# Loads of the first pairs of heads, batch 0: six transfers issued by ScalarE instead of SyncE

## The chip, the cores and the metric

The kernel runs on one core of a Trainium2 chip. The metric is the device time of one execution in microseconds. Before the change the median is 187.37 us over 14 runs (185.96 to 188.53).

The engines are named as in the profile: PE is TensorE (matmuls), DVE is VectorE, ACT is ScalarE, POOL is GpSimd, SP is SyncE. SP computes nothing: it issues transfers. ACT both computes and can issue transfers. Each engine works through its own list of instructions in order; engines wait for each other, and for transfers, on semaphores.

## The reference

Four batches of eight heads of attention, sequence 768, head dimension 64, are followed by a dense block. Some heads ("retrieval") use the full causal mask, the others see only the first 4 keys and a window of 64.

```python
scores = scale * np.matmul(q, k.transpose(0, 1, 3, 2))
stream_keep = causal & (is_sink | in_win)
mask = np.where(retr[0, :, 0, 0, None, None], full_mask, stream_mask)
scores = np.where(mask[None, :, :, :], scores, -1000000000.0)
a = np.exp(scores - max);  a = a / (sum(a) + 1e-09)
attn_out = np.matmul(a, v)
x = attn_out.transpose(0, 2, 1, 3).reshape(B * S, H * D)     # 3072 x 512
h1 = x @ w1;  h2 = x @ w2;  g = np.maximum(h1, h2)           # 512 -> 1024
out = g @ w_out                                              # 1024 -> 512
```

(The lines are shortened; what is computed is unchanged.) The maximum of h1 and h2 is computed in the kernel as h2 + relu(h1 - h2). The part h2 @ w_out is x @ (w2 @ w_out), with the product of the two weights formed once, in the first 40 us or so.

## The kernel before

Heads are first sorted so that the retrieval heads come first; the permutation is computed from `is_retrieval` on DVE and loaded into registers of SP, POOL and ACT, so that a transfer can address "the head in slot s". Heads are then worked on in pairs: four pairs for each of four batches, sixteen rounds in all, numbered r.

For each pair, `pair(b, p)` (from line 658) issues six transfers into three float buffers: q, k and v, each with one transfer for each head. In batch 0 only half of each V is loaded there, because the other half of all heads is fetched at the very start by three transfers from ACT into `v_half` (line 321). A q or k transfer moves 192 KB, a half V transfer 96 KB, and a quarter of a weight 512 KB. After the loads, q and k are cast to bf16 (`qb`, line 301), transposed by PE through PSUM (`mm`, line 695) and copied into `qk` (again line 301). In batch 0 each transposed tile is copied in two halves, one by ACT and one by DVE. V is cast into `vb`. `attend` then makes score tiles on PE (line 578; in batch 0 PE also adds the masks, line 586), exponentials on ACT (line 599), and the product with V on PE (line 623), which DVE normalises. The dense block of a batch (`x_turn`, `dense`) follows its four pairs, interleaved with the next batch's attention.

Weights are loaded by `load_weight` (line 303). `EARLY` names one quarter of w_out that ACT issues at the start (line 324); the other three quarters of w_out and all of w1 and w2 are issued by SP (line 426).

The order of everything is made by a planner in Python, `Plan.schedule`. Each operation has a cost for each engine that may do it, a priority and dependencies; the planner gives every operation an engine and a start time, sorts by start time, and emits each engine's list in that order. The six loads of a pair are operations for the engine "SP" at 0.55 us each. The list of an engine is therefore fixed when the program is built.

Transfers issued by SP and ACT signal their landing on semaphores that are given out in turn from a set of eight. An issue that takes a semaphore over waits on its own engine until the transfer that had it before has landed.

Of the kernel before, what the change touches and what calls it, by code (L numbers as in the profile page):

```python
# [188 lines left out]
def kernel(  # L189
# [19 lines left out]
    nc = tc.nc  # L209
# [87 lines left out]
    def copy(e, o, i):  # L297
        if e == "ACT":
            nc.scalar.copy(out=o, in_=i)  # L299
        else:  # L300
            issued[e].append((V if e == "DVE" else nc.gpsimd).tensor_copy(out=o, in_=i).ins)  # L301
# [75 lines left out]
    def run(full, head, col, exact):  # L377
        P = Plan(*((SHIFT, HOLD) if exact else ({}, {})))
# [276 lines left out]
        def tok(t):  # L655
            return t.rearrange("c (p n) -> c p n", n=NB)

        def pair(b, p):
            r = b * HP + p
            s0 = 2 * p  # L660
            if p == 0:
                xs[b], xt[b], xt_ops[b], norms[b] = Buf(xs_p), Buf(xt_p), [], ([], [])
            raws, loads = [], []
            for i, src in enumerate((q, k, v)):
                t = Buf(ld)
                raws.append(t)
                order, rate = ("(p n)", WIDE) if wide[r] and src is not v else ("(n p)", NARROW)
                two = []
                n0 = NB // 2 if b == 0 and src is v else 0
                for h in range(2):  # L670
                    two.append(P.op(lambda e, t=t, src=src, h=h, order=order, n0=n0: nc.sync.dma_start(
                        out=t.t[:, h, n0:], in_=src[b, bass.ds(head(s0 + h), 1), 128 * n0:].rearrange(
                            f"o {order} d -> p (o n) d", p=128)),
                        {"SP": 0.55}, (), [t], prio=r + 0.01 * i, size=0.0983 if n0 else 0.197, rate=rate))
                loads.append(two)
            qk, vb = Buf(qk_p), Buf(vb_p)
            tk, cast = [], []
            qb = Buf(qb_p)
            for i in range(2):
                one_ = []  # L680
                for hs in ((0,), (1,)) if b == 0 else ((0, 1),):
                    def f(e, i=i, hs=hs):
                        for h in hs:
                            copy(e, qb.t[:, i, :, h, :], raws[i].t[:, h])
                    one_.append(P.op(f, {"POOL": 0.48, "DVE": 0.38} if b == 0 else {"POOL": 0.95},
                                     [loads[i][h] for h in hs], [raws[i], qb], prio=r + 0.01 * i, shared=True))
                cast += one_
                if not wide[r]:
                    continue
                bk = Buf(mm_p)  # L690

                def tr(e, i=i, bk=bk):
                    psb = bk.t[:, 0].bitcast(BF16)
                    for n in range(NB):
                        nc.tensor.transpose(psb[:, n * 128:(n + 1) * 128],  # L695
                                            qb.t[:, i, n].rearrange("p h d -> p (h d)"), ident)
                o = P.op(tr, {"PE": 0.34}, one_, [qb, bk, qk], prio=90 + 2 * r)
                for p0, p1 in ((0, 64), (64, 128)) if b == 0 else ((0, 128),):
                    w = (p1 - p0) / 128
                    tk.append(P.op(lambda e, bk=bk, i=i, p0=p0, p1=p1: copy(  # L700
                        e, tok(qk.t[:, i])[:, p0:p1],
                        bk.t[:, 0].bitcast(BF16)[:, 0:S].rearrange("c (n p) -> c p n", p=128)[:, p0:p1]),
                                   {"DVE": 0.1 + 0.8 * w, "ACT": 0.1 + 0.65 * w}, [o], [bk, qk], prio=r))
            if not wide[r]:
                tk.append(P.op(lambda e: nc.sync.dma_start_transpose(
                    out=qk.t.rearrange("c i (n p) -> c (i n) p", p=128),
                    in_=qb.t.rearrange("p i n h d -> p (i n h d)")),
                    {"SP": XBAR}, cast, [qb, qk], prio=r - 0.5, size=0.393, rate=0.2))
            n0 = NB // 2 if b == 0 else 0
            ov = []  # L710
            if b == 0:
                def fh(e):
                    for h in range(2):
                        copy(e, vb.t[:, h, 0:n0, 0:D], v_half[:, bass.ds(head(s0 + h), 1)].rearrange(
                            "p o (n d) -> p (o n) d", d=D))
                ov.append(P.op(fh, {"POOL": 0.6, "ACT": 0.6}, bufs=[v_held, vb], prio=r + 0.04, ready=DMA_FIRST + 5.2))

            def fv(e):
                for h in range(2):
                    copy(e, vb.t[:, h, n0:, 0:D], raws[2].t[:, h, n0:])  # L720
            ov.append(P.op(fv, {"POOL": 0.58, "DVE": 0.48} if b == 0 else {"POOL": 0.95}, loads[2],
                           [raws[2], vb], prio=r + 0.05, shared=True))

            last[0] = attend(b, p, qk, vb, tk, ov, r)
# [80 lines left out]
        for b in range(B):  # L805
            for p in range(HP):
                pair(b, p)
            x_turn(b)
            dense(b)
# [8 lines left out]
        order = P.schedule()  # L818
# [66 lines left out]
```

The softmax here doesn't subtract the row's maximum and nothing guards it: scores larger than these inputs give would overflow.

## Time and profile before

| | |
|---|---|
| median of 14 runs | 187.37 us |
| profiled execution | 187.53 us |
| its span, first to last instruction | 185.7 us |
| mean granted TensorE clock | 0.970 |
| busy PE / ACT / DVE / POOL | 171.8 / 115.9 / 86.9 / 50.4 us |
| SP: first q load issued, last half V of pair 0 issued | 4.86 us, 8.22 us (end) |
| ACT: three V transfers and one w_out quarter issued | 0.76 to 3.56 us |

Times in the timeline are microseconds from the first instruction of the span: the start, then how long it took, then engine, line and operation, output and input tile, and in brackets the idle time of the engine before it and what ended that. An engine named with a q (SPq, ACTq) is its queue issuing a transfer: the time shown is the issuing, not the transfer. When an operation's bracket names a DMA, its start tells when that transfer had landed. In the table of stages, the clock of PE is a share of its full speed, and the DMA share is how much of the time the core's 16 DMA engines were moving packets.

### The profile page before, as it was taken

The page shows a single profiled execution, that of the slowest core. Times are in us where ns is not written, and L with a number is a line of the kernel's source. Part 1 is how long each engine was busy: PE and PEld are TensorE (multiplying, and loading weights), DVE is VectorE, ACT ScalarE, POOL GpSimd, SP SyncE. Part 2 cuts the span into 40 slices and gives each one's busy share as a digit, 9 for nine tenths or more (in the row PEclk, how much of TensorE's full clock was granted, in tenths as well). Part 3 has the DMA queues.
Part 4 walks back from the last instruction along what each step waited for, and adds up shares of the span by engine and source line. Part 5 has one row for each costly group of instructions (what it writes and reads, how often), then busy time and mean ns, then how long its engine had stood idle before and what let it go on. Part 6 is the DMA issues. An engine that isn't in the chain of part 4 may idle for free.

```text
span 185.7 us, 4614 instructions
## 1 busy us (share of the span) xinstructions
PE 171.8 (93%) x1663; PEld 100.7 (54%) x1663; DVE 86.9 (47%) x250; ACT 115.9 (62%) x195; POOL 50.4 (27%) x108
## 2 busy tenths in 40 slices
PE   0769988899999999999999999999999999999990
PEld 0735754756665655664565456446555545545460
DVE  5647676868678586534378165354743000000000
ACT  2537898978888678817894386368844624426330
POOL 2201151375985764623025234100000000000000
PEclk9965799999999999999999999999999999999999
DMA  6999999999999999999999999982016612022032
GB/s 149 303 278 357 268 308 350 290 311 324 297 291 249 214 236 217 219 238 189 263 247 174 271 219 219 285 223 92 4 58 190 94 60 113 0 79 91 4 113 71
DMA packets 79553, 36.96 MB, mean 199 GB/s; under 512 B 68642, under 2 KB 73506, under 8 KB 79522
## 3 DMA queue, kind: packets, MB, share of 16 engines
q1 hardware_dynamic: 76130, 35.27, 77.3%
q10 hardware_dynamic: 3392, 1.31, 2.6%
q8 instruction: 15, 0.25, 0.6%
q14 instruction: 16, 0.13, 0.2%
HBM read 25.17 MB, written 6.29 MB: 169 GB/s over the span
## 4 chain that ended last, share of the span: by engine, by line
PE 84%; DMA 3%; ACT 3%; DVE 2%; SPq 1%; issue 1%; POOL 0%
PE mm L786 13%; PE mm L762 12%; PE sc L578 9%; PE po L623 9%; PE po L762 8%; PE mm L793 6%; PE po L786 6%; PE sc L786 4%; DMA ld<-in_q_dram 3%; PE mm L463 3%; PE po L793 3%; PE sc L762 2%; PE sc L793 2%; PE mm L695 2%; ACT at_all L599 2%; PE sc L586 2%
## 5 line engine op out<-in xcount | busy, mean ns | idle before, releaser
L599 ACT ACTIVATE at_all<-sc 128x1024 bf16<-128x1024 f32 (+2 forms) x72 | 59.8, 869 | 7.6 <-PE sc L578 3.5
L301 POOL CAST qb<-ld 128x384 bf16<-128x384 f32 x51 | 24.4, 510 | 24.0 <-DVE at_all L610 18.4
L762 PEld LDWEIGHTS <-wd_bf 128*128 128x128 bf16 x256 | 23.2, 98 | 13.8
L623 PE MATMUL po<-vb,at_all 128*128 128x65 bf16 x472 | 26.8, 198 | 0.1
L623 PEld LDWEIGHTS <-at_all 128*128 128x128 bf16 x472 | 22.0, 100 | 9.0 <-issue 1.2
L762 PE MATMUL mm<-xt,wd_bf 128*128 128x384 bf16 x136 | 26.8, 326 | 0.0
L578 PE MATMUL sc<-qk 64*128 64x128 bf16 (+2 forms) x364 | 23.5, 243 | 2.0 <-POOL qk L301 0.8
L642 DVE TENSOR_TENSOR xs<-po,rz 128x192 f32 x64 | 22.9, 357 | 2.9 <-DVE rz L639 0.6
L786 PEld LDWEIGHTS <-raw 128*128 128x128 bf16 x152 | 14.2, 98 | 13.8
L578 PEld LDWEIGHTS <-qk 64*128 64x128 bf16 x364 | 12.7, 95 | 14.9 <-issue 10.2
L301 POOL CAST vb<-ld 128x384 bf16<-128x384 f32 (+1 forms) x30 | 13.5, 479 | 23.3 <-DMA ld<-in_v_dram 9.8
L786 PE MATMUL mm<-wo_bf,raw 128*128 128x512 bf16 (+1 forms) x80 | 19.4, 368 | 0.0
L639 DVE RECIPROCAL rz<-po 128x6 f32<-128x6 f32 x32 | 6.2, 193 | 27.3 <-PE po L623 27.2
L762 PE MATMUL po<-xt,wd_bf 128*128 128x384 bf16 x92 | 18.1, 326 | 0.0
L299 ACT COPY ot<-mm 128x512 f32<-128x512 f32 (+1 forms) x12 | 6.8, 569 | 13.2 <-PE mm L793 11.6
L610 DVE TENSOR_TENSOR at_all<-at_all,smk 128x1024 bf16<-128x1024 bf16 (+3 forms) x27 | 15.0, 574 | 0.0
L793 PEld LDWEIGHTS <-xt 128*128 128x128 bf16 x100 | 9.3, 98 | 9.3
L793 PE MATMUL mm<-wm_bf,xt 128*128 128x512 bf16 (+1 forms) x56 | 13.9, 371 | 0.0
L610 DVE TENSOR_TENSOR at_all<-at_all,tri 128x256 bf16<-128x256 bf16 (+1 forms) x36 | 8.8, 278 | 6.7 <-ACT at_all L599 6.6
L695 PEld LDWEIGHTS <-qb 128*128 128x128 bf16 x108 | 7.5, 105 | 5.3 <-DVE qb L301 3.0
L299 ACT COPY vb<-vb 4x256 bf16<-4x256 bf16 (+1 forms) x16 | 6.1, 380 | 6.2 <-PE po L623 6.1
L770 ACT ACTIVATE raw<-mm 128x384 bf16<-128x384 f32 x17 | 8.4, 491 | 2.5 <-PE mm L762 2.2
(91 smaller groups left out, 190.6 us busy)
## 6 DMA issues: line engine op xcount, KB each, us to landing
ld<-in_q_dram SPq DMA_DIRECT2D x32, 192.0 KB, 4.6
ld<-in_k_dram SPq DMA_DIRECT2D x32, 192.0 KB, 4.7
out_dram<-ot SPq DMA_DIRECT2D x23, 256.0 KB, 2.3
ld<-in_v_dram SPq DMA_DIRECT2D x24, 192.0 KB, 4.5
raw<-in_moe_w_dram SPq DMA_DIRECT2D x8, 512.0 KB, 6.8
raw<-in_moe_w_out_dram SPq DMA_DIRECT2D x3, 512.0 KB, 6.0
xt<-in_v_dram ACTq DMA_DIRECT2D x3, 256.0 KB, 3.3
ld<-in_v_dram SPq DMA_DIRECT2D x8, 96.0 KB, 4.4
```

The lines of the kernel that those rows point to most:

```text
L299: nc.scalar.copy(out=o, in_=i)
L301: issued[e].append((V if e == "DVE" else nc.gpsimd).tensor_copy(out=o, in_=i).ins)
L578: nc.tensor.matmul(sc.t[:, k, off:off + w], lhsT=qk.t[64 * h:64 * h + 64, 1, j * 128:(j + 1) * 128], rhs=qk.t[64 * h:64 * h + 64, 0, q0:q0 ...
L599: nc.scalar.activation(out=a.t[:, k:k + m, 0:n], in_=sc.t[:, k:k + m, 0:n], func=ACT.Exp, scale=scale, bias=0.0 if bias is None else bias[ ...
L610: issued["DVE"].append(V.tensor_mul(out=y, in0=y, in1=z).ins)
L623: nc.tensor.matmul(po[u].t[:, 0, o:o + D + 1], lhsT=a.t[:, k, off + t * 128:off + (t + 1) * 128], rhs=vb.t[:, h, j, :], **fresh(u))
L642: V.tensor_tensor(out=xs[b].t[:, n0:n0 + nn, bass.ds(col(s0 + h), D)], in0=p4[:, i, :, 0:D], in1=rz_[:, i].unsqueeze(2).to_broadcast([128, ...
L695: nc.tensor.transpose(psb[:, n * 128:(n + 1) * 128], qb.t[:, i, n].rearrange("p h d -> p (h d)"), ident)
L762: nc.tensor.matmul(bk.t[:, 0, 0:GT], lhsT=wd_bf[:, c, f * 128:(f + 1) * 128], rhs=xt[b].t[:, g * NB // NG:(g + 1) * NB // NG, c, :], start ...
L770: nc.scalar.activation(out=gt.t[:, f, :], in_=bk.t[:, 0, 0:GT], func=ACT.Relu)
L786: nc.tensor.matmul(bk.t[:, 0, 0:m1 - m0], lhsT=gt.t[:, f, t * 128:(t + 1) * 128], rhs=wo_bf[:, f, m0:m1], start=(f == 0), stop=False)
L793: nc.tensor.matmul(bk.t[:, 0, 0:m1 - m0], lhsT=xt[b].t[:, c0 // 128, c, :], rhs=wm_bf[:, c, m0:m1], start=False, stop=(c == KC - 1))
```

## The change

In batch 0, the two k transfers of pair 0 and the two V transfers each of pairs 0 and 1 are issued by ACT; all other loads of pairs stay with SP. The planner still counts all of them as SP work at 0.55 us, so its plan is the same, and each issue is put into ACT's list where the plan's start time places it. The lines below the edit move by one.

```diff
                 n0 = NB // 2 if b == 0 and src is v else 0
+                queue = nc.scalar if b == 0 and (src is v and p < 2 or src is k and p == 0) else nc.sync
                 for h in range(2):
-                    two.append(P.op(lambda e, t=t, src=src, h=h, order=order, n0=n0: nc.sync.dma_start(
+                    two.append(P.op(lambda e, t=t, src=src, h=h, order=order, n0=n0, queue=queue: queue.dma_start(
                         out=t.t[:, h, n0:], in_=src[b, bass.ds(head(s0 + h), 1), 128 * n0:].rearrange(
                             f"o {order} d -> p (o n) d", p=128)),
                         {"SP": 0.55}, (), [t], prio=r + 0.01 * i, size=0.0983 if n0 else 0.197, rate=rate))
```

The words of the change also name w_out as issued by SyncE. The diff has no line for this: three quarters of w_out were issued by SP before, and the quarter in `EARLY` is issued by ACT before and after.

In ACT's list of the changed program the six issues stand as follows: the two k transfers and the first V transfer of pair 0 come ahead of the conversions of `v_half`; the second V transfer of pair 0 between the conversions for pair 0 and those for another pair, ahead of the conversion of the early w_out quarter; the two V transfers of pair 1 between ACT's copy of its half of the transposed q of pair 0 and its copy of its half of the transposed k of pair 0. The second V transfer of pair 0 takes over the semaphore of the first k transfer; the first V transfer of pair 1 that of the first V transfer of pair 0; the second V transfer of pair 1 that of the w_out quarter which SP issues behind pair 0's q.

## The prediction

> **What bounds the kernel now.** I read the slices of the page first, then busy time by stage, then the timeline of the first 21 us engine by engine, then the waits of the DMA queue and the chain.
>
> ```profile
> PE   0769988899999999999999999999999999999990
> PEclk9965799999999999999999999999999999999999
> DMA  6999999999999999999999999982016612022032
> ```
>
> ```profile
> 5.00:10.00 5.00, 3.71 (x43) 3.36 (x40) 2.90 (x12) 2.49 (x7) 1.08 (x2) 1.00 0.96 292
> 10.00:15.00 5.00, 3.71 (x30) 1.97 (x30) 2.76 (x7) 2.44 (x4) 0.00 (x0) 0.58 0.97 300
> 15.00:20.00 5.00, 4.58 (x50) 3.24 (x48) 3.34 (x9) 3.29 (x4) 1.16 (x3) 0.50 1.08 340
> 20.00:25.00 5.00, 5.00 (x73) 3.53 (x72) 3.74 (x12) 4.64 (x9) 1.74 (x6) 0.90 0.87 236
> 25.00:30.00 5.00, 3.58 (x51) 2.19 (x51) 3.60 (x9) 4.60 (x10) 1.64 (x4) 1.00 1.00 350
> 60.00:100.00 40.00, 40.00 (x431) 22.84 (x430) 23.72 (x66) 28.35 (x49) 16.97 (x37) 1.00 1.13 226
> ```
>
> The columns are PE, PEld, DVE, ACT, POOL busy, then granted clock, DMA share and GB/s. From about 31 us to the end PE never pauses and its order is fixed, so whatever the start loses or gains up to there is paid one for one at the end; nothing behind can absorb it. Between 20 and 30 us ACT is full (9.24 of 10 us). Between 12 and 20 us PE is full at half clock: a mean of 0.58, 0.50 and 0.90 means half clock from 10.8 to 21.0 us. DMA is full from 5 us on.
>
> ```profile
> 2.69 0.87 ACTq L310 DMA_DIRECT2D raw<-in_moe_w_out_dram  x1
> 5.88 1.11 ACT L299 CAST vb<-xt 128x192 bf16 x4 [0.80 <-DMA xt<-in_v_dram]
> 7.73 1.04 ACT L299 CAST wo_bf<-raw 128x1024 bf16<-128x1024 f32 x1 [0.74 <-DMA raw<-in_moe_w_out_dram]
> 9.75 0.48 ACT L299 COPY qk<-mm 128x384 bf16<-128x384 bf16 x1 [0.97 <-PE mm L695]
> 11.49 0.48 ACT L299 COPY qk<-mm 128x384 bf16<-128x384 bf16 x1 [1.26 <-PE mm L695]
> 17.59 1.02 ACT L599 ACTIVATE at_all<-sc 128x1024 bf16<-128x1024 f32 x1 [1.30 <-PE sc L586]
> ```
>
> ```profile
> 9.54 0.36 DVE L301 CAST qb<-ld 128x384 bf16<-128x384 f32 x1 [0.39 <-DMA ld<-in_k_dram]
> 10.27 0.36 DVE L301 CAST qb<-ld 128x384 bf16<-128x384 f32 x1 [0.36 <-DMA ld<-in_k_dram]
> 11.80 0.35 DVE L301 CAST vb<-ld 128x192 bf16<-128x192 f32 x1 [0.44 <-DMA ld<-in_v_dram]
> 14.14 0.69 DVE L301 CAST wo_bf<-raw 128x1024 bf16<-128x1024 f32 x1 [1.53 <-DMA raw<-in_moe_w_out_dram]
> ```
>
> ```profile
> 8.28 0.48 SPq L310 DMA_DIRECT2D raw<-in_moe_w_out_dram  x1
> 14.14 0.90 SPq L671 DMA_DIRECT2D ld<-in_q_dram  x2
> ```
>
> ```profile
> 12.03 0.61 PE L578 MATMUL sc<-qk 64*128 64x384 bf16 x4 [0.57 <-ACT qk L299]
> 15.64 0.82 PE L695 MATMUL mm<-ident,qb 128*128 128x128 bf16 x6 [0.41 <-DVE qb L301]
> ```
>
> A cast that waits for a DMA starts when that DMA lands, so the start times are landings: k of pair 0 at 9.5 and 10.3, V of pair 0 at 11.8, the second w_out quarter at 14.1. ACT copies half of the transposed k at 11.49, and PE's first score waits for it (12.03). The last two SP lines matter most: SP issues the q of pair 2 at 14.14, the moment w_out lands. The built program shows why: its DMAs share eight semaphores in turn, and each issue first waits, on its own engine, until the transfer eight places earlier has landed. On SP such a wait holds up only later loads.
>
> **The change, part by part.** Six issues leave SP for ACT: k of pair 0 (two), V of pair 0 (two), V of pair 1 (two). No issue of w_out moves: three quarters were SP's already, and the fourth stays on ACT. Order of loads, copies and matmuls on PE, DVE and POOL is otherwise unchanged.
>
> *SP, earlier issues.* SP loses 0.92 us (k) and 0.97 us (V) ahead of w_out. It then issues w_out near 6.05 (4.86 plus two q at about 0.6 apart) instead of 8.28, and q of pair 1 behind it. The cover is the DMA share: 0.96 and 0.97 in the two windows from 5 to 15 us. The pipe was full, so an earlier issue moves bytes forward only at other bytes' cost. By rates the most it could win is 292 or 300 to 340 GB/s, 13% of the 8 us up to 14.1, 1.0 us; the least is nothing.
>
> [...]
>
> *ACT, three issues early.* ACT is free at 5.1 (0.80 us idle before 5.88), so it issues both k and one V from about 5.1 to 6.9, at 0.64 us each (three in 1.91 us at its start; SP's take 0.46). The V conversions of 5.88 slip to about 6.9, which needs nothing: they are used by matmuls after 16 us. k now shares the pipe with q instead of following it. Together they are the same four 192 KB transfers, so the last of k still lands near 10.3 (bounds: 9.5 if the pipe gains its 13% and q gets less, 11.3 if w_out behind q takes half the pipe for the last 192 KB and more). I take 10.2, no change.
>
> *ACT, the fourth issue* (second V half of pair 0) reuses the semaphore of the first k half, so ACT waits for that landing, 8.5 to 9.5. Behind it stand two V conversions (0.55 us), the w_out conversion (1.04) and the copy of half of q. With 9.0 + 0.6 + 0.55 + 1.04 the copy starts at 11.2 instead of 9.75. PE does not need it before the k copy is there, so this costs nothing while the next step is later.
>
> *ACT, the fifth and sixth issue* (V of pair 1) stand between the q copy and the k copy of pair 0. The fifth reuses the semaphore of pair 0's first V half, the sixth that of the w_out quarter on SP. So ACT's copy of k, then the first score on PE and all exponentials, wait for w_out. When does it land? Upper bound 14.1: fair sharing must move the same list ahead of its end (the rest of ACT's w_out quarter, q, k, most of V, w_out itself). Lower bound 11.9: 6.05 plus the 5.86 us that it took from 8.28. The list is the same, so I stay near the upper end, less half of the possible rate gain: 13.6. With 0.6 us for the issue the k copy starts at 14.2, not 11.49: **2.7 us late** (bounds 1.0 and 3.2).
>
> *From there to the end.* The first score starts at 12.03 + 2.7 = 14.73. PE runs from 12.03 to 20.2 with one pause, the 0.41 us for q of pair 1 (15.64), which is swallowed: q's casts are done in time. The fourth exponential moves from 17.59 to 19.87 (+2.3). After 21.0 the clock is full, so the fifth (19.02 before) starts at about 21.15 and the sixth (20.20) at 22.2: **+2.0 us**. ACT is full from there to 29.8, then PE to the end: nothing gives it back. With the bounds: 1.0 us late leaves +0.55 (0.41 swallowed); 3.2 us late leaves +2.25.
>
> A clock that returned one step later would keep PE slow and add about 0.6; the row shows the half-clock stretch as one block of 10.2 us, and its end could move by a part of this.
>
> **Sum.** The profiled execution took 187.53 us: span 185.7 and 1.8 around it, 0.16 over the median. 187.37 + 2.0 = **189.4 us**; with the bounds and the clock, 187.9 to 190.2.
>
> **Rivals.**
> (A) V starves, worse. V's rows of 256 B now stand in a second queue beside SP's wide rows. If V's second half lands only with k of pair 1 (whose last cast starts at 16.33 in the timeline), DVE, which converts V ahead of its half of k, copies k at 16.7 to 17.2 instead of 12.07 to 12.62, and the second score tile starts near 17.2 instead of 13.11. Four times 1.02 and 0.38 of exponentials from 18.3 end near 23.4 against 20.58: about +3.0, 190.4; with a late clock 191.4. For it: 11.80 was V's landing behind narrow rows alone. Against it: V is only 192 KB. 20%.
> (B) The wait is short. w_out lands near 12, since SP's queue is served first: +0.4 to +0.8, about 187.9, inside what can't be told from no change. For it: the lower bound. Against it: w_out's bytes follow 384 KB of q, while k and V go on beside it. 15%.
> (C) Faster. The mechanism is the earlier start of k. It decides if both waits on ACT end before k is transposed, w_out landing by 10.8. Then the first score follows k's landing, up to 0.75 us sooner (9.5 against 10.27), and q of pair 1, on the chain until 15.20, lands up to 1.0 sooner: 186.6. Against it: w_out would have to land 3.3 us earlier than now with 2.2 us earlier issue and a full pipe. 8%.
> (D) The listed change does not do all that its words say (w_out stays where it was); that alone costs nothing and is contained in the sum.
>
> **Numbers.** Forecast 57%, A 20%, B 15%, C 8%. Within 0.5%, 0.94 us, a measurement of this kernel can't be told from no change: that is B. Slower is forecast and A, 77%; faster C, 8%. The range runs from 187.7, which takes in most of B, to 191.0, most of A.
>
> **What would show it.** Right: the timeline of ACT has DMA issues between the two qk copies, the second copy starts at 13.6 to 14.7 right after w_out's landing (seen by DVE's w_out cast), the first score near 14.7, and ACT's idle time before the copy goes to a DMA; from 31 us PE is as full as before, 2 us later. Wrong: the second qk copy still near 11.5, or a late start that is made up by 30 us. A shows as a V cast on DVE waiting until about 16.

## The result, and the profile after

| | before | after |
|---|---|---|
| median | 187.25 us (47 runs, 185.96 to 188.89) | 189.24 us (10 runs, 188.66 to 190.27) |
| ratio, 95% interval | | 1.0117 [1.0091, 1.0142] |
| profiled execution, its span | 187.53, 185.7 us | 190.22, 188.3 us |

The change makes the kernel 1.2% slower, 2.0 us. The profiled execution of after lies 1.0 us above its median, so its span grew by 2.6 us where the median grew by 2.0. The ratios leave out executions more than 1.5% above the fastest of their kernel, which bears on two experiments: of the twelve times of k0_v0_copy_first (187.57 to 191.57 us) the upper four are left out, and with all of them the medians are a factor of 1.0096 apart, not 1.0057; of the twelve of only_k0 the highest is left out (188.85 us), and with it the factor is 0.9975, not 0.9963.

First the table of stages of after. The columns are PE, PEld, DVE, ACT, POOL busy (and instructions), granted clock, DMA share, GB/s.

```profile
10.00:15.00 5.00, 1.09 (x12) 0.68 (x12) 1.94 (x6) 1.93 (x5) 0.00 (x0) 0.76 1.04 329
15.00:20.00 5.00, 4.44 (x41) 2.70 (x42) 3.18 (x9) 3.49 (x4) 0.35 (x1) 0.55 0.99 284
20.00:25.00 5.00, 4.86 (x91) 3.67 (x90) 3.98 (x12) 4.79 (x8) 1.55 (x5) 1.00 0.86 214
...
35.00:40.00 5.00, 3.96 (x56) 2.73 (x54) 3.83 (x11) 3.95 (x7) 2.51 (x6) 1.00 0.91 254
```

PE worked 3.71 us between 10 and 15 us before, and 1.09 us now: this is the loss. Two stages hold something else. From 20 us the clock is full, where before it was 0.90 up to 25 us; the half-clock stretch, worked out from the granted clocks of the stages (0.76 and 0.55 here, and 0.60 from 19.25 to 19.5 us; 0.58, 0.50 and 0.90 before), lasts from 12.6 to 19.45 us, against 10.8 to 21.0. And from 35 to 40 us PE is busy 3.96 us where it had been busy 4.96: a second, smaller loss, where the prediction saw none. The row of before for that stage:

```profile
35.00:40.00 5.00, 4.96 (x60) 3.40 (x60) 3.65 (x9) 3.94 (x7) 3.43 (x8) 1.00 1.08 314
```

ACT's timeline of after, over the start:

```profile
5.18 0.96 ACTq L672 DMA_DIRECT2D ld<-in_k_dram  x2
6.41 0.41 ACTq L672 DMA_DIRECT2D ld<-in_v_dram  x1
...
10.06 0.39 ACTq L672 DMA_DIRECT2D ld<-in_v_dram  x1
10.57 0.60 ACT L299 CAST vb<-xt 128x192 bf16 x2 [2.88 <-DMA ld<-in_k_dram]
...
12.03 0.47 ACT L299 COPY qk<-mm 128x384 bf16<-128x384 bf16 x1
14.00 0.96 ACTq L672 DMA_DIRECT2D ld<-in_v_dram  x2
15.00 0.48 ACT L299 COPY qk<-mm 128x384 bf16<-128x384 bf16 x1 [2.50 <-issue]
```

The issue at 10.06 could not go until the first half of k had landed: ACT stands for 2.88 us, and the row names that transfer. The pair of issues at 14.00 waits again, for 1.5 us after the copy of q (12.50). It stands between the two copies of pair 0, so the copy of k starts at 15.00 instead of 11.49. The bracket says "issue", because ACT's last deed before the copy was issuing the DMA; what that issue waited for has to be read from another engine. DVE's timeline of after tells it:

```profile
11.91 0.36 DVE L301 CAST qb<-ld 128x384 bf16<-128x384 f32 x1 [0.39 <-DMA ld<-in_k_dram]
...
14.00 0.35 DVE L301 CAST vb<-ld 128x192 bf16<-128x192 f32 x1 [0.91 <-DMA ld<-in_v_dram]
15.03 0.36 DVE L301 CAST vb<-ld 128x192 bf16<-128x192 f32 x1 [0.67 <-DMA ld<-in_v_dram]
15.51 0.56 DVE L301 COPY qk<-mm 128x384 bf16<-128x384 bf16 x1
```

The first half of V of pair 0 landed when its cast could start, at 14.00, and in the same hundredth of a microsecond ACT's issue goes. So the wait that ended last on ACT was the one for V, whose semaphore the fifth issue takes over. The last row is a second hold: DVE copies its half of k only behind both V casts, and the second V half, issued by ACT at 10.06, came at 15.03. Both halves of k are thus late, for two reasons, and by the same time. PE's timeline of after shows what stood behind:

```profile
15.53 0.61 PE L578 MATMUL sc<-qk 64*128 64x384 bf16 x4 [2.62 <-ACT qk L299]
```

The first score is 3.5 us late (12.03 before). The cast of `wo_bf` on ACT, which comes behind the sixth exponential, starts at 22.25 instead of 20.49, and the exponentials from 23.19 on are 1.5 us late (21.67, 27.86 and 30.65 before; 23.19, 29.40 and 32.19 now). The rest of the loss arises later. First the waits of SP's queue in after's first 40 us (total, times, longest), then the end of the wait in the chain of after, then PE's row of before for the same four transposes (L452):

```profile
SPq L672 <- DMA ld<-in_v_dram: 2.1, 3, 1.1
```

```profile
25.16 11.18 DMA raw<-in_moe_w_dram
36.36 0.70 DVE w_bf L301
37.11 0.40 PE mm L452 x4
```

```profile
35.00 0.40 PE L452 MATMUL mm<-ident,w_bf 128*128 128x128 bf16 x4 [0.42 <-DVE w_bf L301]
```

SP had no wait for a V transfer before. Its issue of q of pair 3 now goes at 19.12 (17.54 before), and its last two w2 quarters start at 24.65 (23.42). These are the quarters that PE transposes (L452) for the product of w2 and w_out. The last one lands at 36.36, where DVE stood 0.48 us for it; before, the last such cast began at 34.26 and did not wait for the transfer, though PE stood 0.42 us for that cast there, too. PE's first product of w2 and w_out (L463) starts 2.1 us late (39.21 against 37.09), and the last matmuls of all, too (182.48 against 180.37). Another 0.5 us of this span lies behind PE's last matmul.

### The profile page after: what moved, and what is told of

Read it like the earlier page. It is cut to its first block, busy times and chain, and to the rows that moved or that the text cites. A ratio compares the mean times of both kernels' runs of the same rounds, so it can differ in the third digit from the quotient of the medians.

```text
span 188.3 us, 4615 instructions
## 1 busy us (share of the span) xinstructions
PE 170.5 (91%) x1663; PEld 100.1 (53%) x1663; DVE 86.7 (46%) x250; ACT 115.6 (61%) x195; POOL 50.0 (27%) x108
## 4 chain that ended last, share of the span: by engine, by line
PE 77%; DMA 6%; DVE 1%; SPq 1%; issue 0%; ACT 0%; DVEq 0%
PE mm L787 12%; PE mm L763 12%; PE po L763 8%; PE po L623 8%; PE sc L578 7%; PE mm L794 6%; DMA raw<-in_moe_w_dram 6%; PE po L787 6%; PE sc L787 4%; PE mm L463 3%; PE po L794 3%; PE sc L763 2%; PE sc L794 2%; PE mm L696 1%; SPq L310 1%; PE po L463 1%
## 5 line engine op out<-in xcount | busy, mean ns | idle before, releaser
L578 PE MATMUL sc<-qk 64*128 64x128 bf16 (+2 forms) x364 | 22.9, 239 | 4.2 <-ACT qk L299 2.6
L623 PE MATMUL po<-vb,at_all 128*128 128x65 bf16 x472 | 26.2, 195 | 0.1
L623 PEld LDWEIGHTS <-at_all 128*128 128x128 bf16 x472 | 21.4, 98 | 8.9 <-issue 1.0
L578 PEld LDWEIGHTS <-qk 64*128 64x128 bf16 x364 | 12.7, 95 | 16.9 <-issue 10.2
```

The source lines that it names most:

```text
L578: nc.tensor.matmul(sc.t[:, k, off:off + w], lhsT=qk.t[64 * h:64 * h + 64, 1, j * 128:(j + 1) * 128], rhs=qk.t[64 * h:64 * h + 64, 0, q0:q0 ...
L623: nc.tensor.matmul(po[u].t[:, 0, o:o + D + 1], lhsT=a.t[:, k, off + t * 128:off + (t + 1) * 128], rhs=vb.t[:, h, j, :], **fresh(u))
```

## The experiments

Some make a part of the change alone, the others take a suspected hold away. In the diffs the line removed is the change's own, or that of the kernel before where the text says so. A median in brackets is that of the kernel before in the same job.

**only_v1: V of pair 1 alone on ACT.**

```diff
-                queue = nc.scalar if b == 0 and (src is v and p < 2 or src is k and p == 0) else nc.sync
+                queue = nc.scalar if b == 0 and (src is v and p == 1) else nc.sync
```

> Of the six moved issues only the two V transfers of pair 1 go to ACT. They stand again between ACT's copies of the transposed q and k of pair 0, but here the semaphores that they take over belong to transfers that have landed before 9 us, so they wait for nothing. Theory (ACT loses time because its issues wait for landings, not because it issues): ACT's k copy stays within 0.3 us of 11.5, ratio to before 0.997 to 1.003. Rival 1 (the issuing itself, about 1 us on ACT, delays the copy): k copy near 12.4, ratio near 1.004 to 1.006.

Measured: 1.0108 [1.0070, 1.0145], median 189.40 us (186.96). Both expectations fell. The copy of k on ACT is on time (11.25) and no DMA is in its bracket, yet the kernel loses about as much as under the whole change. The waits and then the timeline of SP's queue in this kernel:

```profile
SPq L672 <- DMA ld<-in_v_dram: 3.4, 2, 2.4
```

```profile
13.60 3.28 SPq L672 DMA_DIRECT2D ld<-in_q_dram  x2
17.96 0.85 SPq L672 DMA_DIRECT2D ld<-in_k_dram  x2
```

ACT issues the two transfers at 10.25, right behind the copy of q. The turn of the eight semaphores then puts them ahead of later loads of SP, and SP has to wait for them: the second q of pair 2 and the k behind it, which left SP at 14.14 to 16.07 before, leave up to 2.7 us later. All that SP issues afterwards follows late; its first two w2 quarters go at 24.10 (21.86 before), its last two at 25.89. Until then nothing is lost: ACT's exponential at 27.33 is 0.5 us early (27.86 before). Then three engines stand one behind the other, in the timelines of DVE, POOL and PE:

```profile
29.81 0.69 DVE L301 CAST w_bf<-raw 128x1024 bf16<-128x1024 f32 x1 [2.03 <-DMA raw<-in_moe_w_dram]
30.67 0.20 POOL L301 COPY qk<-qk 128x16 bf16<-128x16 bf16 x1 [3.00 <-DVE w_bf L301]
30.92 0.61 PE L578 MATMUL sc<-qk 64*128 64x128 bf16 x8 [2.65 <-POOL qk L301]
```

DVE waits for a w2 quarter, POOL for DVE's cast, PE for POOL's copy. This profile is of an execution of 191.45 us, the longest of this kernel's seven, and PE works at half clock from 30.5 to 37.3 us in it.

**only_v1_wide: the same, but V's rows on ACT are 768 B long instead of 256 B.** V's tokens stand in another order there, so the product with V is not the reference's.

```diff
-                    two.append(P.op(lambda e, t=t, src=src, h=h, order=order, n0=n0, queue=queue: queue.dma_start(
+                    two.append(P.op(lambda e, t=t, src=src, h=h, n0=n0, queue=queue, order="(p n)" if queue is nc.scalar else order: queue.dma_start(
```

> Only the two V transfers of pair 1 on ACT, in 768 B runs (other order of V's tokens in pair 1 of batch 0, output not the reference's there). With 256 B runs this one step cost 1.0108 although ACT's k copy was not late: V took 6.3 and 7.1 us to land and SP's issues, which reuse its semaphores, waited until 16.5 and 18.0. Theory (narrow V is starved and holds SP's queue): V lands by about 15, SP issues k of pair 2 at about 15.5 instead of 17.96, the last weight quarter near 33.5 instead of 35.7; ratio 0.997 to 1.003. Rival (any V of pair 1 on ACT's queue changes the turn of the semaphores, and that is the loss): ratio 1.007 to 1.013.

Measured: 1.0103 [1.0057, 1.0148], median 189.88 us (187.39). The width of the rows does not matter here. SP's second q of pair 2 still waits, to about 15.5, and the k behind it goes at 16.73 (15.22 before). Its w2 quarters are late again (the last two at 25.61), and PE stands 2.39 us for POOL's copy at 30.61. With only_v1 this says that the hold on SP is there at either width, and that it costs about 1% by itself.

**k0_and_v0: all of the change but V of pair 1.**

```diff
-                queue = nc.scalar if b == 0 and (src is v and p < 2 or src is k and p == 0) else nc.sync
+                queue = nc.scalar if b == 0 and (p == 0 and (src is v or src is k)) else nc.sync
```

> k and V of pair 0 on ACT, V of pair 1 back on SP: ACT has no issue between its q copy and k copy. Theory with two causes (a wait on ACT, and V's narrow rows starving in the second queue, which holds DVE's k copy because DVE converts V first): ACT's k copy comes at about 13, but DVE's V conversion still waits until about 15 and DVE's k copy starts near 15.5; loss about half of the change's, ratio 1.004 to 1.008. Rival (all of the loss is ACT's wait at the V issues of pair 1): ratio within 0.998 to 1.003. Rival (all of it is pair 0's transfers): ratio 1.009 or more.

Measured: 1.0114 [1.0068, 1.0160], median 189.42 us (186.96): more than expected, and no less than the whole change. ACT's copy of k came 2.07 us earlier than in after (12.93), and the first score with it (13.46). But DVE's timeline reads:

```profile
14.99 0.36 DVE L301 CAST vb<-ld 128x192 bf16<-128x192 f32 x1 [0.92 <-DMA ld<-in_v_dram]
15.26 0.55 DVE L301 COPY qk<-mm 128x384 bf16<-128x384 bf16 x1
```

The other half of k waits behind V, and the matmuls of the second score tile that need it start only at 15.86. Of two holds on the same tile one had been taken away, and the other is left. Here the loss lies in the start alone: DVE waits for no w2 quarter, and PE's first product of w2 and w_out starts 1.3 us late.

**change_copy_first: the change, with DVE's copy of k put ahead of its V casts.**

```diff
+            if r == 0:
+                P.moved = ov[-1], tk[-2:]
...
+        conversion, copies = P.moved
+        order.remove(conversion)
+        order.insert(max(order.index(o) for o in copies) + 1, conversion)
```

> The whole change with the same exchange on DVE. Theory (two holds lie on top of each other: ACT's k copy waits at 15.0 for V and w_out, DVE's k copy waits for V at 15.0; taking away DVE's alone leaves ACT's): ACT's k copy stays near 15.0, first score near 15.5; ratio 1.008 to 1.014. Rival (DVE's hold is the one that counts): ratio 1.000 to 1.006.

Measured: 1.0137 [1.0085, 1.0189], median 189.85 us (187.38). Here the V casts no longer stand ahead of DVE's copy and ACT's hold is left. The timelines of ACT and DVE:

```profile
14.01 0.94 ACTq L672 DMA_DIRECT2D ld<-in_v_dram  x2
14.99 0.48 ACT L299 COPY qk<-mm 128x384 bf16<-128x384 bf16 x1 [3.37 <-DMA ld<-in_v_dram]
...
15.50 0.56 DVE L301 COPY qk<-mm 128x384 bf16<-128x384 bf16 x1 [2.76 <-ACT qk L299]
```

ACT's copy is where it was in after, and this time the bracket itself names V. DVE's copy, free of V, now waits for ACT's copy, and is where it was in after, too: the hold on ACT alone makes both halves late. The first score is at 15.52. Nothing is gained.

**k0_v0_copy_first: both holds taken away** (the same edit, on k0_and_v0).

```diff
-                queue = nc.scalar if b == 0 and (src is v and p < 2 or src is k and p == 0) else nc.sync
+                queue = nc.scalar if b == 0 and (p == 0 and (src is v or src is k)) else nc.sync
...
+        conversion, copies = P.moved
+        order.remove(conversion)
+        order.insert(max(order.index(o) for o in copies) + 1, conversion)
```

> k and V of pair 0 on ACT, as in the run that cost 1.0114, but DVE copies its half of the transposed k of pair 0 before it converts V of pair 0. Theory (in that run V's second half, landing at 15.0, held DVE's k copy until 15.3 and the second score tile until 15.9, and that is most of the loss): DVE's k copy follows ACT's at about 13.4, the second score tile about 14.6; ratio 1.001 to 1.007. Rival (the loss is elsewhere, in SP's queue or the later loads): ratio stays at 1.009 to 1.014.

Measured: 1.0057 [1.0018, 1.0097], to be read with the other figure given under the result, 1.0096. In the timeline it does what it should: DVE's copy of k starts at 13.13, three exponentials run without a pause from 14.34, and V's late second half (15.48) now delays only pair 1 behind it (the fourth exponential stands 1.56 us and starts at 18.97). That both holds have to go is seen in the traces; whether half of the loss goes with them or hardly any of it, these times do not settle.

**only_k0 and only_v0.**

```diff
-                queue = nc.scalar if b == 0 and (src is v and p < 2 or src is k and p == 0) else nc.sync
+                queue = nc.scalar if b == 0 and (src is k and p == 0) else nc.sync
```

> Only k of pair 0 on ACT. Nothing on ACT waits for a landing, and V stays on SP's queue behind q, beside k. Theory: q and k share the pipe, q lands 0.5 to 1 us later, k within 0.7 us of before, V not later than 13; ratio 0.997 to 1.004. Rival (the sharing of q and k is itself the loss, since q is delayed past 10.9 as in the whole change): ratio 1.005 or more. Rival (the earlier start of k is a gain): 0.996 or less.

Measured: 0.9963 [0.9930, 0.9995], median 186.50 us (186.96). In its profile the first score is later than before (13.60), but the six exponentials from 14.79 follow without a pause. The profile gives the clock as full from 10 to 20 us; yet four score matmuls take 0.61 us at 13.60, as at half clock before (12.03), and 0.39 at 17.33, so that reading is not to be relied on. What brings the 0.4% is not settled, and with all twelve times the difference is smaller still (0.9975).

```diff
-                queue = nc.scalar if b == 0 and (src is v and p < 2 or src is k and p == 0) else nc.sync
+                queue = nc.scalar if b == 0 and (src is v and p == 0) else nc.sync
```

> Only the two V transfers of pair 0 on ACT; they wait for no landing and start behind ACT's own early w_out quarter, beside q on SP's queue. Theory (narrow rows in one queue get a small share beside wide rows in the other): V lands at 12 to 15 although it is issued 1.5 to 2 us earlier, later than the 11.8 of before, q and k a little earlier; DVE's V conversion then delays its k copy; ratio 1.000 to 1.006. Rival (the queues share by bytes): V lands by 9.5, k up to 0.7 us later, ratio 0.998 to 1.003, k copy on ACT up to 12.2.

Measured: 1.0047 [1.0020, 1.0074], median 187.75 us (186.96). V is not starved here: both casts follow each other from 12.29 without a wait for a DMA. It is k's second half that comes late, 11.55 against 10.27, and ACT's copy of k with it (12.83). Two things now go out earlier beside k: V on ACT, from 5.19, and w_out on SP, at 7.13 instead of 8.28. Whether either of them delays k was not tested.

**change_wide_v: the change with V's rows on ACT 768 B long** (the edit of only_v1_wide, and like there V's tokens stand in another order).

> The whole change, but the four V transfers on ACT's queue read three tokens side by side for each partition (768 B runs instead of 256 B; same bytes, same buffers), so the tokens of V stand in another order and the output of batch 0 is not the reference's. Theory (narrow rows on the second queue get a small share beside wide rows on SP's, V lands late, and by the shared semaphores both ACT and SP wait for it): V of pair 0 lands by about 12 instead of 13.9 and 15.0, ACT's k copy is set by w_out's landing, 12.8 to 13.6, SP is no longer held by V of pair 1; ratio to before 1.000 to 1.006. Rival (the loss comes from ACT's waits whatever the width, or from q and k sharing the pipe): ratio stays at 1.008 to 1.014.

Measured: 1.0074 [1.0040, 1.0108], median 189.17 us (187.39). V lands earlier (its second half 14.19 instead of 15.03), ACT's issue goes at 12.23 and its bracket names w_out as the wait that ended last; the copy of k is at 13.15, and SP's q of pair 3 at 16.71 is no longer held. The narrow rows are a part of the loss, perhaps 0.4%; the two intervals overlap a little.

**only_early_wout_on_sp: before, with the early w_out quarter issued by SP; and change_and_early_wout_on_sp.** In the first the line stands against the kernel before; in the second the change is made, too.

```diff
-            load_weight(name, c, nc.scalar)
+            load_weight(name, c, nc.sync)
```

> The kernel before with one change that the words of the edit name and its diff does not make: the early quarter of w_out is issued by SP, ahead of pair 0's q, and ACT's queue holds only the first halves of V (narrow). If wide rows go ahead of narrow ones in another queue, this quarter lands by about 5 instead of 7.7, q and k of pair 0 then land 0.5 to 1.5 us earlier, the first halves of V later (7 to 9, which holds ACT's and POOL's conversions of them, needed only after 16): ratio 0.992 to 1.000. Rival (ACT, which converts the first halves of V ahead of its q copy, now waits for them past 10): ratio 1.002 to 1.010.

Measured: 0.9982 [0.9955, 1.0010], median 187.10 us (187.39): no difference that can be told. The loads of k land earlier, their casts at 8.97 and 9.56 instead of 9.54 and 10.27.

> The whole change, and the early quarter of w_out issued by SP too, as the words of the edit can be read. Theory: ACT's queue now holds the first halves of V, k of pair 0 and V, so k stands behind narrow rows that share with SP's wide ones, and ACT's waits for V remain: ACT's k copy at 14 to 16; ratio 1.006 to 1.016. Rival (the early quarter on ACT's queue was what made k and V late): ratio 0.996 to 1.003.

Measured: 1.0086 [1.0053, 1.0119], median 188.99 us (187.38). V's halves land 0.9 and 0.6 us earlier (13.11 and 14.40), but the hold stays: ACT's copy of k is at 14.08 with V named in its bracket.

**k0_and_early_wout_on_sp: k of pair 0 on ACT, the early w_out quarter on SP, nothing of V moved** (against the kernel before: the edits of only_k0 and only_early_wout_on_sp).

```diff
-            load_weight(name, c, nc.scalar)
+            load_weight(name, c, nc.sync)
...
+                queue = nc.scalar if b == 0 and (src is k and p == 0) else nc.sync
```

> The two edits that did not lose, together: k of pair 0 on ACT, early w_out quarter on SP. Theory A (gains add): ratio 0.990 to 0.997. Theory B (k now stands behind the first halves of V, 256 B rows, and q behind w_out's wide rows, so k lands at 10 to 12 and the first score is later than with the w_out edit alone): ratio 0.998 to 1.006. B is likelier.

Measured: 0.9926 [0.9896, 0.9957], median 186.00 us (187.38): faster than both kernels. ACT's timeline:

```profile
10.17 1.03 ACT L299 COPY qk<-mm 128x384 bf16<-128x384 bf16 x2 [0.40 <-PE mm L696]
...
12.02 3.07 ACT L599 ACTIVATE at_all<-sc 128x1024 bf16<-128x1024 f32 x3 [0.81 <-PE sc L586]
...
15.84 2.22 ACT L599 ACTIVATE at_all<-sc 128x1024 bf16<-128x1024 f32 x3 [0.74 <-PE sc L586]
```

ACT copies both halves one behind the other with no issue between them, and is through the sixth exponential at 18.06 (20.58 before). From 10 to 20 us the pipe moves 343 GB/s (320 before), w_out's second quarter lands by 12.42 (14.14), and the last w2 quarter by 31.90.

**before_again: the kernel before, profiled once more.**

> The kernel before once more, for its profile: does the half-clock stretch (10.8 to 21.0 us in the first profile) lie at the same place in each execution? Theory: the same landings within 0.5 us, a stretch that may start elsewhere, be shorter, or be missing, with a span within 1 us of 185.7. Rival: the stretch is the same in each execution, so the differences of clock between the kernels' profiles are effects of the edits.

Measured: 186.56 us, span 184.8. Its stage from 10 to 20 us:

```profile
10.00:20.00 10.00, 8.58 (x95) 5.30 (x92) 6.58 (x17) 6.40 (x9) 1.15 (x3) 0.66 1.03 320
```

The clock was 0.54 in the same stage of the first profile. The half-clock stretch lasts 6.8 us here (11.7 to 18.6) and 10.2 us there, in one and the same kernel, and the span differs by 0.9 us. The first score is 0.2 us earlier than there, the exponential behind the `wo_bf` cast 0.95 us (20.72 against 21.67), and so are the last matmuls (179.47 against 180.37). So a span of a single execution is no measure of an edit in this study, and the verdicts above rest on the timed ratios.

## Why the prediction was right, and where not

**The mechanism** was right for the start: the issues stand in ACT's list between its two copies, they wait for earlier transfers, and the first score waits for the second copy. ACT's issues at 14.00, the copy at 15.00 and the score at 15.53 show it, and change_copy_first names V in the bracket.

**SP's earlier issue, "nothing".** The pipe was full as reckoned (DMA share 1.04 from 10 to 15 us). w_out landed earlier, at 12.8 against 14.1, but q and k of pair 0 landed later: q's first cast starts at 9.68 (8.31 before), and the last half of k, taken as unchanged at 10.2, landed at 11.91, above its upper bound of 11.3. The later holds covered this.

**The fourth issue, "costs nothing".** Wrong. It held ACT to 10.06, which put the copy of q at 12.03 (11.2 forecast), still without harm. But it also let the second V half start only then, so that V landed at 15.0, and DVE has that cast ahead of its copy of k. The prediction had this hold as a rival's alone (A, with V near 16). In k0_and_v0, where this hold is left and ACT's second one is not, the kernel loses as much as under the whole change; its k is late, too (first score 1.4 us late), so the hold's own share is not known.

**The fifth and sixth issue.** This is the term that was mis-sized. The forecast let w_out end the wait, landing at 13.6, and the copy of k start 2.7 us late, with an upper bound of 3.2. The fair sharing that its bound for w_out supposes was the author's assumption, and no run shows it. The runs showed 3.5 us. w_out, issued by SP at 5.98, had landed 6.8 us later, at 12.8; the first V half took until 14.00, and issuing the pair took 0.96 us where 0.6 was reckoned. V's rows of 256 B are a part of it: in change_wide_v, with 768 B, the wait ended at 12.23, by w_out.

**From there to the end.** The forecast gave back 0.7 of its 2.7 us by 22 us and nothing later. Measured against the profile of before, 2.0 of 3.5 us were given back by 23 us, 0.41 of it for the pause that was swallowed. That leaves 1.5, not 2.0. But the half clock ended at 19.45 in after and at 21.0 in that profile. Against before_again, whose half-clock stretch is as long as after's, the first score is 3.7 us late (15.53 against 11.81) and the exponential of 23.19 is 2.5 us late (20.72 there). So 1.5 or 2.5 are left, by the profile taken for before, and 2.0 lies between them. The 0.6 us that the range holds for a clock returning one step later was the author's estimate, and no run shows it; before and before_again, with 10.2 and 6.8 us at half clock, differ by 0.9 us of span.

**"From 31 us PE is as full as before."** Wrong: PE was busy 3.96 us from 35 to 40 us. The text had said that such waits on SP hold up only later loads, and then did not price one of them, the last w2 quarter. It had also read that PE never pauses from about 31 us on, while PE's row of before has a pause of 0.42 us at 35.00, for the cast of that quarter. ACT's V transfers entered SP's turn, and 0.6 us more were lost at 36.36 (1.5 late before, 2.1 behind it); against before_again it is 0.5 (2.5 and 3.0).

The sum, 2.0, agrees with the measured 2.0 us, and luck has a part in it. The 0.5 to 0.6 us lost at 36 us were not in the sum, so the start must have cost less than the forecast said, by about as much, in the median execution. That is an inference: single profiles of before differ by 0.9 us of span, as much as the errors in question.

**The rivals.** A, V behind wide rows, holds in part: V did end both waits, but at 14.0 and 15.0, not 16, and only_v0 shows V in time when it is issued from 5.19 on (cast from 12.29, without a wait). A's own sum does not come out as written: four times 1.02 and 0.38 from 18.3 end at 22.8, and at 23.3 with the two pauses of before (0.41 and 0.16), 2.8 us late, not 3.0. B and C fell with w_out no longer the last. What did not occur among the rivals is the third hold, on SP. It is the largest single finding of the experiments: only_v1 loses 1.1% with ACT's copies on time. The parts do not add up (1.1% for V of pair 1 alone, 1.1% for the rest, 1.2% for both), so they may delay the same work at different places, and how much of the 2.0 us belongs to each in the full change stays open.

Moving issues from one engine to the other changed the time in both directions: 1.0117 with k and V on ACT, 0.9926 with k on ACT and the early w_out quarter on SP.

## What to carry to other kernels

In this kernel an issue on ACT is an instruction in ACT's list with a wait of its own (in after 2.88 us of idle time before the cast at 10.57, 2.50 before the copy at 15.00): before moving one, look up which transfer's semaphore it takes over, when that lands, and what stands behind it on the engine. Then look at the other side of the turn: who takes over the moved transfer's semaphore, and what that queue has to issue later (in only_v1 SP's k of pair 2 left at 17.96 instead of 15.22). Prefer to move a load whose semaphores are free (here k of pair 0, with the early w_out quarter on SP: 0.9926), and if taking one hold away changes nothing, look for a second one on the same tile before giving up the theory.

## What was not expected of the hardware

The half-clock stretches in the first 40 us, worked out from the granted clocks of the stages, last 10.2 us (before, k0_and_v0, k0_v0_copy_first), 6.8 (after, before_again, only_v1_wide and others) or 3.4 (k0_and_early_wout_on_sp), and only_v1 has two of 6.8: one, two or three times 3.4 us. The same kernel got two in one execution and three in another, at 0.9 us of span. What sets the 3.4 us, and how many of them a stretch takes, no run here shows.

Moving one 512 KB quarter of w_out from ACT to SP, and nothing else, brought the casts of k forward by 0.6 to 0.7 us, while the time hardly moved (0.9982).
